# The first gate one piece later, two gates beside the fourth piece, and gate weights converted at half the rate, in a kernel of attention, Fourier mixing and two MLP stages

## The chip, the cores and the metric

The kernel runs on one core of one Trainium2 chip. The metric is device time in microseconds: 626.51 us as the median of 3 runs before the change (622.10 to 628.71). A core has TensorE (PE in the rows; its weight loads are PEld), VectorE (DVE), ScalarE (ACT), GpSimd (POOL) and SyncE (SP), each with an instruction queue of its own that it works off in order, and DMA engines that copy between HBM and the on-chip memory.

## The reference

Three blocks in a row, all in float32. For a batch of 4, with 768 time steps t:

```python
# 1. gated linear attention, 8 heads of 48
state = alpha[:, :, t, :, None] * state + einsum('bhd,bhe->bhde', k[:, :, t], v[:, :, t])
y[:, :, t] = einsum('bhd,bhde->bhe', q[:, :, t], state)
# 2. Fourier mixing and an MLP, d_model 384, hidden 1536
u = x + real(fft(fft(x, axis=1), axis=2))
un = (u - mean(u)) / sqrt(var(u) + 1e-06)
x = u + maximum(un @ w_ch1, 0) @ w_ch2
# 3. a convolution of 5 taps over time gates a value
gate = sigmoid(sum_k conv_w[k] * x shifted by k)
out = (gate * (x @ w_val)) @ w_out
```

## The kernel before, in words

**Tiling.** Attention is computed in chunks of 128 time steps, 6 chunks for each of the 4 batches. The MLP and the gate work on pieces of 256 time steps, 3 a batch, 12 in all; this text counts the pieces from the first to the twelfth. Products in the MLP and the gate are made in three parts (a high and a low part of each operand, function `mm3`, L646 to L648), so every weight is held as two arrays, and every activation is split by a copy on ScalarE and a subtraction on VectorE or GpSimd.

**Weights.** They arrive as 64-bit floats in blocks of 384 columns. `weight_parts` turns a block into its two arrays with three integer instructions on VectorE (L222, L225, L229), a copy on ScalarE (L233) and a subtraction (L238 on VectorE; in the head TensorE and ScalarE do it, L242 to L244). 24 blocks belong to the MLP; then come the convolution's taps and 6 blocks of the gate's two matrices. They pass through a buffer (`arena`) that the second batch's u takes over later.

**The head.** `first` runs the attention of the first batch and the conversion of weights in an order written by hand: one string of letters for each of 8 steps (`FIRST`), where A, B, U, S, D are parts of a chunk, w a part of a conversion, l loads, 0 to 2 the transposes of x, f to h the folds ahead of the Fourier transform, and p, r its first two parts. Then the transform of the first batch (`dft`) and the norm of its first piece.

**The main loop** (`run`) goes through the pieces. `mlp` is a generator of 24 steps: it makes the hidden layer in six pairs of 128 columns and works the second product in one pair later; each pair is evicted by ScalarE (hh, L667) and VectorE (hlo, L669). At every step the loop lets the side work go one step further (`tick`): the norm of the next piece from step 10 on, and the gate of the piece before. It also converts a weight block every second step, advances the background (`back`: attention and transform of the next batch, some 91 steps spread over a batch's three pieces by `PACE`, the parts of a chunk at the places of the letters in `ORDER`), and issues the range checks of the inputs (`check`). What is left of the gate at the end of a piece is run out before the next piece begins.

**The gate** of a piece closes the MLP (L702, L708: the product by the inverse deviation, the addition to u), splits x (L712, and L727 on GpSimd), makes the 15 taps on VectorE (L719, L721), the sigmoid on ScalarE (L729), 27 value products on TensorE, the product with the gate (L741), its split (L742 on ScalarE, L743 on GpSimd), 18 output products (L757), and two stores. It also waits until all weights are converted. The tile `ga` that holds the gate exists once.

**Attention of a chunk.** `attn_a` scans alpha on VectorE (L288 to L298), `attn_b` transposes and makes the scores on TensorE (L310, L318) with a mask (L319), `attn_c` updates the state (L335, L341 to L348), `attn_d` makes the output (L362, L368), which reads a value tile va that SyncE loads ahead (L273).

Of the kernel before, what the change touches and what calls it, by code (L numbers as in the profile page):

```python
# [9 lines left out]
F32 = mybir.dt.float32  # L10
# [3 lines left out]
AF = mybir.ActivationFunctionType  # L14
ALU = mybir.AluOpType
# [4 lines left out]
P, C = 128, 64  # L20
NT = S // P
NP = H // 2
KC = 5
NK = 256
NPC = S // NK
NF = DFF // P
KD = DM // P
# [3 lines left out]
N_CHECK = 768  # L31
N_FLAGS = 48
CHECK_FROM = 1
CHECK_STEP = 6
W_SCALE = 2.0**20
RS_SCALE = 1.3541813492306554 * 2.0**62
DEFER = 2
LAG_BG = 6
SOON = 2
BG_FROM = 5  # L40
LAG_US = 5
LAG_SS = 5
LAG_RS = 3
FIRST = ("lAwlwwlql", "llBwwlaAUSvqwll", "BwAwDwlUaqSvll", "BlwwAlwwallDUvSq", "wAylDlBwaUSwxv", "BAllUSlDlwawv", "BawDllU0lSww1lfl", "lDg2wlllplhrl")
ORDER = ".BAab..Dt..mCvc.q."
PACE = (1, 0.8, 0.95, 1.15, 0.85, 0.65, 0.95, 1.1, 1.2, 1, 1, 1)
BG_STEPS = 91
TICKS = 24
N_NORM = 10
W_DFT = (2, 0, 2, 0, 0, 0, 0, 0, 0, 1, 0)  # L50
W_CAP = 2
N_EARLY, N_SOON, N_JOBS = 18, 24, 31


# [10 lines left out]
class Main:  # L65
# [388 lines left out]


    def fold_open(self, b):
        self.us[b] = u = self.t([P, KD, S + KC - 1], "u", 2)
        self.nc.gpsimd.memset(u[:, :, 0 : KC - 1], 0.0)
        self.eo = [self.t([P, 3, 2, 193], "w", 5) for _ in range(2)]
# [228 lines left out]
        self.ch[(b, p)] = ch  # L688


    def gate(self, b, p):
        nc = self.nc
        rs = self.nm[(b, p)][2]
        ch = self.ch.pop((b, p))
        u = self.us[b]
        o = p * NK
        x2 = u[:, :, KC - 1 + o : KC - 1 + o + NK]
        gs = self.t([P, KD, NK], "ga", 1)
        tms = []
        for j in range(KD):  # L700
            tm = gs[:, j]
            nc.vector.tensor_tensor(out=tm, in0=ch[j], in1=rs, op=ALU.mult)  # L702
            tms.append(tm)
            if j == 1:
                yield
        for j in range(KD):
            eng = nc.gpsimd if b * NPC + p in ADD_POOL else nc.vector
            eng.tensor_tensor(out=x2[:, j], in0=x2[:, j], in1=tms[j], op=ALU.add)  # L708
            if j == 0:
                yield  # L710
        xh = self.pair(b * NPC + p + 2, [P, KD, NK])
        nc.scalar.activation(out=xh, in_=x2, func=AF.Copy)  # L712
        yield
        for k in range(KC):
            for j in range(KD):
                xs = u[:, j, o + k : o + k + NK]
                w = self.cw[:, j, k : k + 1]
                if k == 0:
                    nc.vector.tensor_scalar(out=gs[:, j], in0=xs, scalar1=w, scalar2=None, op0=ALU.mult)  # L719
                else:  # L720
                    nc.vector.scalar_tensor_tensor(out=gs[:, j], in0=xs, scalar=w, in1=gs[:, j],  # L721
                                                   op0=ALU.mult, op1=ALU.add)
            yield
            if k == 1:
                xl = self.pair(b * NPC + p + 2, [P, KD, NK])
                eng = nc.gpsimd if b * NPC + p in XL_POOL else nc.vector
                eng.tensor_tensor(out=xl, in0=x2, in1=xh.bitcast(F32), op=ALU.subtract)  # L727
                yield
        nc.scalar.activation(out=gs, in_=gs, func=AF.Sigmoid)  # L729
        yield  # L730
        while self.weights_left(False):
            self.weight_step()
            for _ in range(4):
                self.weight_load(True)
        gh = self.pair(b * NPC + p + 3, [P, KD, NK])
        gl = self.pair(b * NPC + p + 3, [P, KD, NK])
        for j in range(KD):
            va = self.aux()
            for k in range(KD):
                self.mm3(va[:, :NK], self.wv, slice(j * P, (j + 1) * P), (xh[:, k], xl[:, k]), k, k == 0, k == KD - 1)  # L740
            nc.vector.tensor_tensor(out=gs[:, j], in0=va[:, :NK], in1=gs[:, j], op=ALU.mult)  # L741
            nc.scalar.activation(out=gh[:, j], in_=gs[:, j], func=AF.Copy)  # L742
            nc.gpsimd.tensor_tensor(out=gl[:, j], in0=gs[:, j], in1=gh[:, j].bitcast(F32), op=ALU.subtract)  # L743
            yield
        if self.tail and b * NPC + p + 2 == B * NPC:
            self.rest = (b, p, gh, gl)
            return
        yield
        yield
        os = gs.rearrange("p a b -> p (a b)").rearrange("p (a b) -> p a b", b=DM)  # L750
        for t in range(NK // P):
            ts = slice(t * P, (t + 1) * P)
            po = self.aux()
            n = 0
            for k in range(KD):
                for lh, rh in ((gh, self.wo[0]), (gh, self.wo[1]), (gl, self.wo[0])):
                    nc.tensor.matmul(out=po[:, :DM], lhsT=lh[:, k, ts], rhs=rh[:, k, :], start=n == 0, stop=n == 8)  # L757
                    n += 1
            ob = os[:, t]
            nc.scalar.activation(out=ob, in_=po[:, :DM], func=AF.Copy)  # L760
            nc.sync.dma_start(out=self.ap["out"][b * S + o + t * P : b * S + o + (t + 1) * P, :], in_=ob)
            yield
# [115 lines left out]
    def run(self):  # L878
# [12 lines left out]
        nc = self.nc  # L891
# [18 lines left out]
        acc = 0.0  # L910
        pieces = [(b, p) for b in range(B) for p in range(NPC)]

        def tick():
            for s in list(side):
                if next(s, self) is self:
                    side.remove(s)

        for i, (b, p) in enumerate(pieces):
            n = 0
# [22 lines left out]
                tick()  # L942
            while gating and gating[0] in side:
                tick()
            self.gated = i
            if i + 1 < len(pieces):
                gating = [self.gate(b, p)]
                side.extend(gating)
        for _ in checking:
            pass  # L950
# [95 lines left out]
    def general(self, ctx):  # L1046
        nc = self.nc
        self.tail = False
        with ExitStack() as c:
            self.pools(c, "ww")  # L1050
            self.any_weights()
        xp = ctx.enter_context(self.tc.tile_pool(name="xp", bufs=1))
        self.x = xp.tile([P, NT, DM + 2], F32, name="general_x")
        self.heads = xp.tile([P, 2], F32, name="heads")
        nc.vector.memset(self.heads, 0.0)
        for j in range(2):
            nc.vector.memset(self.heads[j * 64 : j * 64 + 64, j : j + 1], 1.0)
        for b in range(B):
            with ExitStack() as c:
                self.pools(c, f"sc{b}")  # L1060
                self.scanned(b)
            with ExitStack() as c:
                self.pools(c, f"wk{b}")
                for _ in self.dft(b, False):
                    pass
                for p in range(NPC):
                    for step in (self.norm, self.mlp, self.gate):
                        for _ in step(b, p):
                            pass


@with_exitstack
# [90 lines left out]
```

## Time and profile before

| | before |
|---|---|
| median of 3 runs | 626.51 us |
| profiled execution | 625.92 us, span 624.1 us |
| TensorE busy | 584.7 us (94%) |
| VectorE busy | 409.9 us (66%) |
| ScalarE busy | 241.9 us (39%) |
| GpSimd busy | 156.3 us (25%) |
| granted clock, mean | 0.974 |

The shares are means over the span, and its stretches differ: the head with the first attention, the first two pieces with conversions beside them, the pieces with a background, and the last ones without. Where VectorE or TensorE is full is read from stretches of the trace. [...]

### The profile page before, as it was taken

To read this page: it belongs to the slowest core of one execution; us is meant where nothing else is said; L and a number is where in the kernel's file an instruction comes from. 1 tells how busy PE (TensorE), PEld (TensorE's weight loads), DVE (VectorE), ACT (ScalarE), POOL (GpSimd) and SP (SyncE) were. 2 spreads that over 40 slices of the span, in tenths; PEclk is the share of its full clock that TensorE was granted. 3 is DMA by queue.
4 is the path that set the end of the run, shared out by engine and by line. 5 is a ranking of instruction groups with operands and counts; after the bars stand their busy time and mean duration, and the time that the engine had idled before them with its cause. 6 is when DMAs were issued, how large, how long until landed. Compare 5 with 4: busy or idle time off the path is not lost.

```text
span 624.1 us, 15821 instructions
## 1 busy us (share of the span) xinstructions
PE 584.7 (94%) x6636; PEld 548.7 (88%) x6636; DVE 409.9 (66%) x881; ACT 241.9 (39%) x553; POOL 156.3 (25%) x331
## 2 busy tenths in 40 slices
PE   3788999887999998999999999999999999999996
PEld 2567888786999898999999999899998999999995
DVE  7988689999435756965753938877554536272634
ACT  2334432224453263353443243333444344435332
POOL 0010024131234043222331231322231223223130
PEclk9968998799999999999999999999999999999999
DMA  8865344573133244534313236344311122242301
GB/s 345 287 217 183 110 153 81 161 197 103 53 127 98 77 127 124 166 99 76 126 57 98 77 127 148 90 154 79 123 51 35 52 58 54 77 60 77 60 3 56
DMA packets 29601, 69.44 MB, mean 111 GB/s; under 512 B 5200, under 2 KB 15952, under 8 KB 29520
## 3 DMA queue, kind: packets, MB, share of 16 engines
q1 hardware_dynamic: 29520, 68.33, 37.6%
q8 instruction: 54, 0.88, 0.6%
q14 instruction: 27, 0.22, 0.1%
HBM read 63.59 MB, written 4.73 MB: 109 GB/s over the span
## 4 chain that ended last, share of the span: by engine, by line
PE 74%; DVE 16%; DMA 3%; POOL 2%; ACT 2%; issue 2%; SPq 0%; DVEq 0%; POOLq 0%; ACTq 0%
PE mm L646 7%; PE ch L646 7%; PE ch L647 7%; PE mm L647 7%; PE ch L648 7%; PE mm L648 7%; PE aux L757 5%; PE aux L509 4%; PE aux L554 3%; PE aux L318 2%; DVE w L295 2%; DVE w L288 2%; PE aux L646 2%; PE aux L647 2%; PE aux L648 2%
## 5 line engine op out<-in xcount | busy, mean ns | idle before, releaser
L646 PE MATMUL mm<-hl,w1h 128*128 128x256 f32 x432 | 129.6, 300 | 1.0 <-ACT hl L603 1.0
L646 PE MATMUL ch<-hh,w2h 128*128 128x256 f32 x432 | 129.7, 300 | 0.2 <-ACT hh L667 0.2
L648 PE MATMUL ch<-hlo,w2h 128*128 128x256 f32 x432 | 122.3, 283 | 1.5 <-DVE hlo L669 1.5
L648 PE MATMUL mm<-hl,w1h 128*128 128x256 f32 x432 | 123.3, 285 | 0.0
L647 PE MATMUL mm<-hl,w1l 128*128 128x256 f32 x432 | 123.2, 285 | 0.0
L647 PE MATMUL ch<-hh,w2l 128*128 128x256 f32 x432 | 122.2, 283 | 0.0
L669 DVE SCALAR_TENSOR_TENSOR hlo<-mm,hh 128x512 fp32r<-128x512 f32 x72 | 49.6, 689 | 100.7 <-ACT hh L667 100.4
L646 PEld LDWEIGHTS mm<-hl,w1h 128*128 128x128 f32 x432 | 83.3, 193 | 4.0 <-ACT hl L603 1.4
L646 PEld LDWEIGHTS ch<-hh,w2h 128*128 128x128 f32 x432 | 82.3, 190 | 2.8 <-ACT hh L667 0.4
L647 PEld LDWEIGHTS mm<-hl,w1l 128*128 128x128 f32 x432 | 83.6, 193 | 0.8
L648 PEld LDWEIGHTS mm<-hl,w1h 128*128 128x128 f32 x432 | 83.7, 194 | 0.3 <-DVE hl L606 0.3
L648 PEld LDWEIGHTS ch<-hlo,w2h 128*128 128x128 f32 x432 | 81.5, 189 | 1.9 <-DVE hlo L669 1.9
L647 PEld LDWEIGHTS ch<-hh,w2l 128*128 128x128 f32 x432 | 81.7, 189 | 0.9
L667 ACT ACTIVATE hh<-mm 128x512 fp32r<-128x512 f32 x72 | 42.6, 591 | 71.4 <-PE mm L648 71.4
L721 DVE SCALAR_TENSOR_TENSOR ga<-u,cw,ga 128x256 f32<-128x256 f32 x132 | 54.9, 476 | 0.0
L743 POOL TENSOR_TENSOR hl<-ga,hl 128x256 fp32r<-128x256 f32 x33 | 26.6, 811 | 93.2 <-ACT hl L742 92.0
L375 POOL COPY x<-x 128x2 f32<-128x2 f32 x24 | 12.6, 527 | 137.2 <-ACT x L374 137.2
L612 POOL TENSOR_TENSOR tmp<-tmp,tmp 128x256 f32<-128x256 f32 x24 | 18.1, 755 | 72.2 <-ACT tmp L611 71.3
L318 PEld LDWEIGHTS aux<-w 48*64 48x64 f32 x768 | 26.2, 144 | 9.9 <-issue 4.0
L757 PE MATMUL aux<-wvo,hl 128*128 128x384 f32 x180 | 34.8, 336 | 0.0
L318 PE MATMUL aux<-w 48*64 48x64 f32 x768 | 29.6, 231 | 4.9 <-DVE w L298 2.9
L727 POOL TENSOR_TENSOR hl<-u,hl 128x768 fp32r<-128x768 f32 x11 | 20.2, 1840 | 45.0 <-ACT hl L712 41.8
(181 smaller groups left out, 1157.6 us busy)
## 6 DMA issues: line engine op xcount, KB each, us to landing
qka<-in_qka_dram SPq DMA_DIRECT2D x23, 770.5 KB, 5.7
ck<-in_w_dram SPq DMA_DIRECT2D x24, 384.0 KB, 3.3
vu<-in_vu_dram SPq DMA_DIRECT2D x24, 192.0 KB, 3.7
u<-in_w_dram SPq DMA_DIRECT2D x12, 384.0 KB, 6.0
va<-in_va_dram SPq DMA_DIRECT2D x24, 192.0 KB, 4.1
ck<-in_al_dram SPq DMA_DIRECT2D x12, 384.0 KB, 3.5
out_dram<-ga SPq DMA_DIRECT2D x22, 192.0 KB, 1.8
w<-in_cs_dram SPq DMA_DIRECT2D x6, 579.0 KB, 5.6
```

The lines of the kernel that those rows point to most:

```text
L318: nc.tensor.matmul(out=sc[j * 64 : j * 64 + 64, cs], lhsT=kt[hs, cs], rhs=qt[hs, cs], start=True, stop=True)
L509: self.nc.tensor.matmul(out=pa[: d1 - d0, g * 193 : g * 193 + n], lhsT=self.eo[g][:, t, m, d0:d1], rhs=self.cs[g][:, t, m, :n], start=t == ...
L554: nc.tensor.matmul(out=pa[:, :385], lhsT=self.cd[:w, dt, mi, kt * P : (kt + 1) * P], rhs=pq[:w, mi, dt, :], start=dt == 0, stop=dt == 1)
L646: nc.tensor.matmul(out=out, lhsT=w[0][:, k, cols], rhs=xh, start=first, stop=False)
L647: nc.tensor.matmul(out=out, lhsT=w[1][:, k, cols], rhs=xh, start=False, stop=False)
L648: nc.tensor.matmul(out=out, lhsT=w[0][:, k, cols], rhs=xl, start=False, stop=last)
L667: nc.scalar.activation(out=hh, in_=hp, func=AF.Relu)
L669: nc.vector.scalar_tensor_tensor(out=hl, in0=hp, scalar=0.0, in1=hh.bitcast(F32), op0=ALU.max, op1=ALU.subtract)
L721: nc.vector.scalar_tensor_tensor(out=gs[:, j], in0=xs, scalar=w, in1=gs[:, j], op0=ALU.mult, op1=ALU.add)
L727: eng.tensor_tensor(out=xl, in0=x2, in1=xh.bitcast(F32), op=ALU.subtract)
L743: nc.gpsimd.tensor_tensor(out=gl[:, j], in0=gs[:, j], in1=gh[:, j].bitcast(F32), op=ALU.subtract)
L757: nc.tensor.matmul(out=po[:, :DM], lhsT=lh[:, k, ts], rhs=rh[:, k, :], start=n == 0, stop=n == 8)
```

## The change

`gate` is cut in two. `close` does the end of the MLP (L702, L708) beside the next piece as before. The rest, still called `gate`, is run by a table, `PLAN`: beside the second piece none, beside the third the first piece's gate, beside the fourth those of the second and the third piece, and from then on each beside the piece that follows, as before. The second of two gates makes its three value tiles first and splits them together at the end. Before the second batch's transform opens, all weights are converted. The intervals change: `DEFER` (steps between two conversions of the gate's blocks) from 2 to 4, `SOON` (the same for the MLP's last blocks) from 2 to 3, and several lags, the places in `ORDER`, the weights in `PACE` and the strings of `FIRST`.

```diff
-CHECK_STEP = 6
+CHECK_STEP = 5
-DEFER = 2
+DEFER = 4
-SOON = 2
+SOON = 3
-LAG_US = 5
+LAG_US = 4
-LAG_RS = 3
+LAG_RS = 4
...
-ORDER = ".BAab..Dt..mCvc.q."
-PACE = (1, 0.8, 0.95, 1.15, 0.85, 0.65, 0.95, 1.1, 1.2, 1, 1, 1)
+ORDER = ".BAab.D.t..Ccmq.v."
+PACE = (1, 0.6, 0.95, 1.2, 0.95, 0.7, 0.9, 1.1, 1.3, 1, 1, 1)
-W_DFT = (2, 0, 2, 0, 0, 0, 0, 0, 0, 1, 0)
+W_DFT = (2, 0, 1, 0, 1, 0, 0, 0, 0, 1, 0)
+PLAN = {1: (), 2: (0,), 3: (1, 2)}
...
     def fold_open(self, b):
+        while b == 1 and self.tail and self.weights_left(False):
+            self.convert_one()
...
-    def gate(self, b, p):
+    def close(self, b, p):
...
+    def gate(self, b, p, r, second=False):
+
+        nc = self.nc
+        u = self.us[b]
+        o = p * NK
+        x2 = u[:, :, KC - 1 + o : KC - 1 + o + NK]
+        gs = self.t([P, KD, NK], "ga", 1)
+        xh = self.pair(r + 1 + second, [P, KD, NK])
...
-        gh = self.pair(b * NPC + p + 3, [P, KD, NK])
-        gl = self.pair(b * NPC + p + 3, [P, KD, NK])
+            self.convert_one()
+        gh, gl = (None, None) if second else (self.pair(r + 2, [P, KD, NK]) for _ in range(2))
...
-            nc.scalar.activation(out=gh[:, j], in_=gs[:, j], func=AF.Copy)
-            nc.gpsimd.tensor_tensor(out=gl[:, j], in0=gs[:, j], in1=gh[:, j].bitcast(F32), op=ALU.subtract)
-            yield
+            if second:
+                yield
+                if j < KD - 1:
+                    continue
+                gh, gl = (self.pair(r + 2, [P, KD, NK]) for _ in range(2))
+            for i in range(KD) if second else (j,):
+                nc.scalar.activation(out=gh[:, i], in_=gs[:, i], func=AF.Copy)
+                nc.gpsimd.tensor_tensor(out=gl[:, i], in0=gs[:, i], in1=gh[:, i].bitcast(F32), op=ALU.subtract)
+                yield
...
+        def after(r):
+            yield from self.close(*pieces[r - 1])
+            for n, i in enumerate(PLAN.get(r, (r - 1,))):
+                yield from self.gate(*pieces[i], r, n > 0)
+                self.gated = i + 1
+
...
-            self.gated = i
             if i + 1 < len(pieces):
-                gating = [self.gate(b, p)]
+                gating = [after(i + 1)]
```

**Where instructions move.** On VectorE, in the second piece, between its second and third eviction of the hidden layer, there stood before (ga is the first gate's tile, w, qka, sp and st are tiles of the attention, u a staged weight block there where it is written to wvo, hlo the eviction):

```order
L669 SCALAR_TENSOR_TENSOR hlo_1768<-mm_1705,hh_1766 128x512
L719 TENSOR_SCALAR ga_1650<-u_469,cw 128x256 x3
L298 TENSOR_TENSOR w_1732<-qka_1518,w_1731 128x512
L721 SCALAR_TENSOR_TENSOR ga_1650<-u_469,cw,ga_1650 128x256 x3
L238 TENSOR_TENSOR wvo_1059<-u_103,wvo_1059 128x384
L343 TENSOR_TENSOR sp_1862<-st_1684,pend_1553 128x192
L345 TENSOR_TENSOR sp_1862<-aux_1842,sp_1862 128x192
L348 TENSOR_TENSOR st_1865<-aux_1843,sp_1862 128x192
L721 SCALAR_TENSOR_TENSOR ga_1650<-u_469,cw,ga_1650 128x256 x3
L669 SCALAR_TENSOR_TENSOR hlo_1894<-mm_1868,hh_1892 128x512
```

Now, between the same two evictions (the lines of the changed kernel are 1 to 3 higher here):

```order
L672 SCALAR_TENSOR_TENSOR hlo_1704<-mm_1681,hh_1702 128x512
L289 SCALAR_TENSOR_TENSOR w_1713<-qka_1513,ends 128x516
L293 RECIPROCAL starts<-w_1713 128x4
L294 TENSOR_TENSOR w_1714<-qka_1513,w_1713 128x512
L296 SCALAR_TENSOR_TENSOR w_1713<-qka_1513,starts 128x516
L320 TENSOR_TENSOR w_1706<-aux_1721,mask 128x512
L223 TENSOR_SCALAR u_103<-u_103 128x384
L226 SCALAR_TENSOR_TENSOR u_103<-u_103 128x384
L230 SCALAR_TENSOR_TENSOR u_103<-u_103 128x384
L239 TENSOR_TENSOR wvo_1072<-u_103,wvo_1072 128x384
L299 TENSOR_TENSOR w_1714<-qka_1513,w_1713 128x512
```

The taps of the gate are gone from here; a scan and a whole conversion stand in their place, which before stood ahead of the first of these rows.

On TensorE, where the third piece's gate ends, there stood before, in the middle of the next piece (mm and ch are products of the MLP, the tile wvo,hl rows the gate's output products):

```order
L648 MATMUL mm_3501<-hl_408_2807,w1h 128x256
L757 MATMUL aux_3524<-wvo_1059,hl_477_3322 128x384 x2
L757 MATMUL aux_3524<-wvo_1059,hl_478_3323 128x384
L757 MATMUL aux_3524<-wvo_1059,hl_477_3322 128x384 x2
L757 MATMUL aux_3524<-wvo_1059,hl_478_3323 128x384
L757 MATMUL aux_3524<-wvo_1059,hl_477_3322 128x384 x2
L757 MATMUL aux_3524<-wvo_1059,hl_478_3323 128x384
L596 MATMUL aux_3536<-tmp_3337,avg 128x256
```

The first of the output products now follow the gate's value products (hl,wvo) at once:

```order
L649 MATMUL aux_3834<-hl_515_3543,wvo_1072 128x256
L650 MATMUL aux_3834<-hl_515_3543,wvo_1072 128x256
L651 MATMUL aux_3834<-hl_532_3664,wvo_1072 128x256
L771 MATMUL aux_3855<-wvo_1072,hl_549_3845 128x384 x2
L771 MATMUL aux_3855<-wvo_1072,hl_550_3846 128x384
```

Before, products of the MLP stood between the values and the outputs of a gate; now, for this one gate, none do, and the next piece's MLP comes behind all 18 output products.

## Rows read from the trace of the kernel before

**Rows 1.** Busy time by stretch: start:end, length, engines, granted clock, DMA share, GB/s.
```profile
core 0: us, PE busy (x) PEld busy (x) DVE busy (x) ACT busy (x) POOL busy (x), PEclk, DMA share, GB/s
0.00:88.40 88.40, 67.70 (x934) 53.33 (x934) 71.67 (x153) 32.63 (x80) 7.15 (x22) 0.90 0.65 228
88.40:163.00 74.60, 64.81 (x905) 60.29 (x906) 69.03 (x139) 23.93 (x53) 22.53 (x40) 0.91 0.43 117
163.00:293.40 130.40, 127.89 (x1648) 120.49 (x1647) 78.48 (x165) 56.32 (x122) 40.28 (x84) 1.00 0.38 108
293.40:603.80 310.40, 309.72 (x3063) 300.59 (x3060) 180.59 (x401) 124.25 (x286) 86.35 (x186) 1.00 0.31 82
```

**Rows 2.** TensorE's waits, 88.4 to 163 us: total us, times, longest.
```profile
PE aux L335 <- ACT x L373: 3.3, 2, 2.4
PE aux L318 <- DVE w L602: 2.0, 1, 2.0
PE aux L362 <- DMA va<-in_va_dram: 1.7, 1, 1.7
```

**Rows 3.** VectorE's time line, 138 to 165 us: start, duration, instruction.
```profile
139.54 0.35 DVE L222 TENSOR_SCALAR u<-u 128x384 int32<-128x384 int32 x1
139.93 0.56 DVE L225 SCALAR_TENSOR_TENSOR u<-u 128x384 int32<-128x384 int32 x1
...
141.47 1.23 DVE L288 TENSOR_TENSOR_SCAN w<-qka,ends 128x516 f32<-128x516 f32 x1
...
145.73 1.37 DVE L719 TENSOR_SCALAR ga<-u,cw 128x256 f32<-128x256 f32 x3
147.02 0.68 DVE L298 TENSOR_TENSOR w<-qka,w 128x512 f32<-128x512 f32 x1
147.62 1.27 DVE L721 SCALAR_TENSOR_TENSOR ga<-u,cw,ga 128x256 f32<-128x256 f32 x3
148.81 0.55 DVE L238 TENSOR_TENSOR wvo<-u,wvo 128x384 fp32r<-128x384 f32 x1
...
158.29 0.68 DVE L298 TENSOR_TENSOR w<-qka,w 128x512 f32<-128x512 f32 x1
...
160.08 0.41 DVE L741 TENSOR_TENSOR ga<-aux,ga 128x256 f32<-128x256 f32 x1
```

**Rows 4.** A gate's end: groups of 163 to 293.4 us, and the chain.
```profile
L742 ACT ACTIVATE hl<-ga 128x256 fp32r<-128x256 f32 x8 | 3.3, 411 | 5.8 <-DVE ga L741 5.8
L743 POOL TENSOR_TENSOR hl<-ga,hl 128x256 fp32r<-128x256 f32 x8 | 6.6, 831 | 18.3 <-ACT hl L742 18.3
171.00 1.57 PE aux L757 x9
```

**Rows 5.** The chain of waits, 60 to 90 us: start, us, what.
```profile
61.16 0.68 PE aux L468 x6
...
62.46 0.54 PE aux L368 x32
...
64.57 1.30 PE mm L509 x8
```

**Rows 6.** VectorE beside GpSimd: time lines, and all taps (ns min/median/max).
```profile
114.15 1.74 POOL L612 TENSOR_TENSOR tmp<-tmp,tmp 128x256 f32<-128x256 f32 x2 [12.19 <-ACT tmp L611]
114.32 0.97 DVE L225 SCALAR_TENSOR_TENSOR u<-u 128x384 int32<-128x384 int32 x1
L721 DVE SCALAR_TENSOR_TENSOR ga<-u,cw,ga x132: 469/476/482, 147.6 to 590.5; 128x256 f32<-128x256 f32 x132
```

**Rows 7.** The value load: issues (count, KB, median us to landing), and the chain.
```profile
va<-in_va_dram SPq DMA_DIRECT2D x24, 192.0 KB, 4.1
238.37 6.20 DMA va<-in_va_dram
```

More of the change, by code (lines that the diff above doesn't have):

```diff
@@ L33 @@
 CHECK_FROM = 1
-CHECK_STEP = 6
+CHECK_STEP = 5
 W_SCALE = 2.0**20
 RS_SCALE = 1.3541813492306554 * 2.0**62
-DEFER = 2
+DEFER = 4
 LAG_BG = 6
-SOON = 2
+SOON = 3
 BG_FROM = 5
-LAG_US = 5
+LAG_US = 4
 LAG_SS = 5
-LAG_RS = 3
-FIRST = ("lAwlwwlql", "llBwwlaAUSvqwll", "BwAwDwlUaqSvll", "BlwwAlwwallDUvSq", "wAylDlBwaUSwxv", "BAllUSlDlwawv", "BawDllU0lSww1lfl", "lDg2wlllplhrl")
-ORDER = ".BAab..Dt..mCvc.q."
-PACE = (1, 0.8, 0.95, 1.15, 0.85, 0.65, 0.95, 1.1, 1.2, 1, 1, 1)
+LAG_RS = 4
+FIRST = ("llAwlwwlqlll", "lllBwllwAaUqSvwl", "wBAwDwllUlalvqSl", "lBwAwwallvDUSq", "wAyDlBwaUSwxvl", "BUwAlllllSlDwvaw", "lBaDUwll0lSww1f", "Dgllpwll2lhlr")
+ORDER = ".BAab.D.t..Ccmq.v."
+PACE = (1, 0.6, 0.95, 1.2, 0.95, 0.7, 0.9, 1.1, 1.3, 1, 1, 1)
 BG_STEPS = 91
@@ L710, in gate @@
                 yield
-        xh = self.pair(b * NPC + p + 2, [P, KD, NK])
+    def gate(self, b, p, r, second=False):
[5 more added lines that the diff above has]
+        xh = self.pair(r + 1 + second, [P, KD, NK])
         nc.scalar.activation(out=xh, in_=x2, func=AF.Copy)
@@ L724, in gate @@
             if k == 1:
-                xl = self.pair(b * NPC + p + 2, [P, KD, NK])
+                xl = self.pair(r + 1 + second, [P, KD, NK])
                 eng = nc.gpsimd if b * NPC + p in XL_POOL else nc.vector
@@ L731, in gate @@
         while self.weights_left(False):
-            self.weight_step()
-            for _ in range(4):
-                self.weight_load(True)
-        gh = self.pair(b * NPC + p + 3, [P, KD, NK])
-        gl = self.pair(b * NPC + p + 3, [P, KD, NK])
+            self.convert_one()
+        gh, gl = (None, None) if second else (self.pair(r + 2, [P, KD, NK]) for _ in range(2))
         for j in range(KD):
@@ L1066, in general @@
                 for p in range(NPC):
-                    for step in (self.norm, self.mlp, self.gate):
+                    for step in (self.norm, self.mlp, self.close):
                         for _ in step(b, p):
                             pass
+                    for _ in self.gate(b, p, b * NPC + p + 1):
+                        pass
 @with_exitstack
```

## The prediction

> **What bounds the kernel now.** I read the busy time by stretch first, with the span cut where the program changes its nature [rows 1]. From 293.4 to 603.8 us TensorE is busy 309.72 of 310.4 us at granted clock 1.00: nothing can be gained there by moving work, only lost. From 163.0 to 293.4 us it is still TensorE, 127.89 of 130.4 us, with VectorE at 78.48. Between 88.4 and 163.0 us it is the other way round: VectorE is busy 69.03 of 74.6 us, TensorE 64.81 at a mean clock of 0.91. That is the first piece of the MLP and two thirds of the second, where VectorE has the weights of the gate to convert, the scans of the second batch's attention and the first gate. The head before 88.4 us is mixed, TensorE 67.70 and VectorE 71.67 of 88.4.
>
> Then the waits of TensorE in the middle stretch [rows 2]: 3.3 us for ScalarE to free a bank of PSUM, 2.0 us for VectorE in one transposed product, 1.7 us for a load. The waits are small because TensorE reaches most of them late. What is long is VectorE's own queue: its time line [rows 3] stands without a gap from 138 to 160 us while a weight, a scan and a tap of the convolution take turns.
>
> So there is work that can move: VectorE is full until 163 us and 60% busy (78.48 of 130.4) in the next stretch, while TensorE is the bound there. I sum against the profiled execution, 625.92 us with a span of 624.1; the median of the three runs, 626.51, lies 0.6 above it.
>
> **What leaves the stretch from 88.4 to 163.0 us.** I cut both orders at the same place, the fourth eviction of the second piece's hidden layer, and count VectorE's instructions before it. Missing after the change are:
> - the first gate's 15 taps and one product with its values. Three first taps start at 145.73 and the next instruction at 147.02, 1.29 us; three later ones take 147.62 to 148.81, 1.19 us, four times [rows 3]. With the product, 0.4 us, 6.5 us.
> - three weight blocks and one more subtraction, since a block is now converted every fourth step of the MLP, not every second. A block runs from 139.54 to 141.47, 1.93 us [rows 3]; the subtraction is a quarter of it: 6.3 us.
> - the end of one attention chunk (one product, three state updates), 158.29 to 160.08, 1.8 us [rows 3], because the background is paced slower there.
>
> Together 14.6 us, 33 instructions of 138. None disappears; all stand again between there and the first eviction of the fifth piece. VectorE would be busy 54.4 us. If its idle share of today stays (74.6 - 69.03 = 5.6 us) the stretch lasts 60.0 us.
>
> TensorE has 64.81 us there less what leaves it, 9 products of the gate and 16 small ones of the attention, 1.8 us: 63.0 us, if its clock falls as often as now. If it never fell, 64.81 x 0.91 - 1.8 = 57.2 us would do. On the other side, the waits of TensorE that no VectorE work causes, 3.3 and 1.7 us [rows 2], come on top of 63.0: 68.0. **I take 63.0**, TensorE's own work at today's clock, since it lies above VectorE's 60.0 and is made of the row nearest to it. That is 11.6 us less than 74.6, with 57.2 to 68.0 as ends (17.4 and 6.6 less).
>
> The clock first as the rows have it: mean 0.91 where TensorE waits for VectorE, 1.00 in the two stretches where it is 98% and 99.8% busy [rows 1]. [...]
>
> **What arrives from 163.0 to 293.4 us.** VectorE gets 78.48 + 14.6 = 93 us in some 132: covered by TensorE, at no cost. TensorE gets its 1.8 us back, and it is the bound: **+1.8 us**.
>
> **Where the cover is thin: the end of the fourth piece.** Its side work is now one closing, one gate and a second gate, 35 steps against the 24 of a piece. The rest is run out with no MLP work between. The order shows it: the second gate's 27 value products and the 18 output products stand back to back. Between them ScalarE must copy (0.41 us) and GpSimd subtract three times (0.83 us each) [rows 4], 2.9 us to the last piece, and the last of the first nine output products needs it. Nine take 1.57 us [rows 4]; so 2.9 + 0.17 - 1.57, **+1.5 us** of TensorE idle. Below, nothing, if GpSimd's tiles come while TensorE is still at the values. Above: VectorE may be late with the taps ahead of it.
>
> [...] Beside GpSimd's two additions at 114.15 us a VectorE instruction of the conversion took 0.97 us; the same one at 139.93, alone, 0.56 [rows 3, 6]. The taps never did so: 132 of them lie between 469 and 482 ns [rows 6], but almost none runs beside a GpSimd addition today. [...] If it held for all twelve two-input taps of the second gate, they would take 12 x 0.40 x (0.97 / 0.56 - 1) = 3.5 us more. [...]
>
> **The head.** One group of transposes now stands behind the first eight products of the Fourier transform, not ahead of them. They waited for the last attention chunk's evictions: TensorE leaves that chunk at 63.0 (62.46 + 0.54) and starts the transform at 64.57 [rows 5]. Starting it at once gives 1.57; the six transposes, 0.68 [rows 5], then stand inside: **-0.9 us**, on the chain. The other head edits (a state product ahead of weight products, a mask product behind a conversion) let VectorE run ahead and then wait for TensorE elsewhere; I take 0, and 1.5 us either way.
>
> **Edits at nothing.** The number of the range checks, of the norms' additions and of the background's steps is unchanged; their new places lie under TensorE's 309.72 of 310.4 us [rows 1]. The value load of the attention is issued four background steps ahead of its use, not five. If that cover went, TensorE would wait in each chunk; priced below.
>
> **Sum:** -11.6 + 1.8 + 1.5 - 0.9 = -9.2; 625.92 - 9.2 = **616.7 us**.
>
> **The rivals.**
> 1. *The bound only changes hands.* TensorE and VectorE come out nearly equal (63.0 and 60.0), and each waits for the other in turn: a scan for a product, a product for an eviction. Then the stretch takes 68.0, the piece's end 5.0 and the head nothing: 625.92 - 6.6 + 1.8 + 5.0 = 626.1. For it: the waits there today are of that kind [rows 2]. Against: today VectorE has only 5.6 us of idle time in 74.6 with such dependences. Half of the 9.4 us between this and the forecast already gives 621. Within 1%.
> 2. *The clock holds too.* 57.2 us instead of 63.0: 616.7 - 5.8 = 610.9. For it, the 1.00 of the full stretches [rows 1]. Against, the clock also fell where TensorE was mostly busy.
> 3. *Slower: the value load comes late.* It is landed 4.1 us after its issue in the median, but 6.2 us in the longest link of the chain [rows 7], where TensorE waited; 91 steps are spread over three pieces, some 140 us, so a step is about 1.5 us, the lead falls from 7.6 to 6.1 us, and SyncE issues in order behind other waits. If all 18 background chunks lost 1.5 us, it would cost 27 us: 644. From 0.9 us a chunk (16 us in all) the kernel is over 1% slower. Against: the median leaves 2 us, and of the waits of today only the longest loads are left.
> 4. *The conversion is not really deferred*: the program must finish all weights before the second batch's transform opens, since they share a buffer. The order shows one block left to force there, 2 us at most, so this only shades rival 1.
>
> **Chances.** A change below 1%, 6.3 us, cannot be told from none here: faster means below 620.2, slower above 632.8. The forecast, 613 to 620: 0.54. Rival 2, below 613: 0.18. Rival 1 with the part of 4, 620 to 633: 0.21. Rival 3: 0.07. So faster 0.72, same 0.21, slower 0.07. The range: from the sum with 57.2 us and 1.5 us more from the head, 609, to rival 1 at 626; below and above lie some 2 in 10. The likeliest cases' own range, forecast and rival 2, is 609 to 620.
>
> **What would show it.** In the profile of the changed kernel: the stretch from the first hidden eviction to the tenth near 63 us with VectorE near 54; TensorE's share there above 95% and no half clock for much longer than now; at the end of the fourth piece a wait of 1 to 2 us of the output products for GpSimd's subtraction; the transform starting some 1.5 us earlier than the transposes before it allow today; waits for the value load no more than 5 us in all. Wrong would be: TensorE idle for VectorE in the second piece as before, waits for the value load in most chunks, or more than 5 us of idle time where the fifth piece starts.

## The result, and the profile after

The changed kernel takes 616.83 us (median of 4 runs, 613.6 to 618.44) where the kernel before took 625.51 beside it: a ratio of 0.984, 95% interval 0.980 to 0.988. Timed once more in the third study below it had 614.06 us and 0.981, 0.978 to 0.984. The forecast was 616.7 us, faster. The profiled execution took 617.39 us with a span of 615.6.

Busy time by stretch, cut at the same places of the program as [rows 1] (start:end, length, TensorE, weight loads, VectorE, ScalarE, GpSimd, granted clock, DMA share, GB/s). The granted clock is the share of its full clock that the profile records as granted to TensorE; in the traces of both kernels every record of it is 1.00 or 0.50, and 0.50 is what half clock means here.

```profile
core 0: us, PE busy (x) PEld busy (x) DVE busy (x) ACT busy (x) POOL busy (x), PEclk, DMA share, GB/s
0.00:86.30 86.30, 63.37 (x934) 50.55 (x934) 71.54 (x152) 32.64 (x81) 7.73 (x22) 0.94 0.67 234
86.30:149.00 62.70, 57.12 (x877) 53.97 (x881) 54.64 (x106) 20.23 (x48) 19.48 (x38) 0.95 0.43 126
149.00:285.80 136.80, 132.79 (x1693) 124.69 (x1684) 96.13 (x198) 61.76 (x134) 47.49 (x85) 0.99 0.40 118
285.80:595.10 309.30, 309.14 (x3053) 300.14 (x3053) 177.56 (x401) 118.66 (x279) 87.62 (x186) 1.00 0.27 78
```

The second line is the one to read: 62.70 us where there were 74.6, and VectorE at 54.64 where there were 69.03. The third line gives half of that back: 136.80 for 130.4, with TensorE at 132.79 for 127.89.

TensorE's waits in the second stretch, which answer to [rows 2] (total us, times, longest):

```profile
PE aux L363 <- DMA va<-in_va_dram: 2.5, 1, 2.5
PE aux L319 <- DVE w L299: 1.9, 1, 1.9
PE aux L363 <- DVE sp L342: 1.1, 1, 1.1
```

The longest is now a load (va, the values of the attention), which had 1.7 us in this stretch before [rows 2]. What the clock does behind it is seen in two cuts of the busy time:

```profile
121.00:130.50 9.50, 7.69 (x113) 7.19 (x112) 9.19 (x20) 2.58 (x7) 2.21 (x5) 1.00 0.64 113
130.50:137.40 6.90, 6.22 (x84) 6.16 (x85) 5.10 (x9) 2.35 (x6) 1.76 (x3) 0.51 0.55 211
```

TensorE waits from 128.7 to 131.2 us; at 130.5 us the granted clock falls from 1.00 to 0.50 and stays there for 6.8 us. The products of the MLP start 0.21 us apart in that time and 0.12 us apart right behind it.

The end of the double gate on TensorE and GpSimd, which answers to [rows 4] (start, us, instruction, idle time before it):

```profile
277.56 0.62 PE L771 MATMUL aux<-wvo,hl 128*128 128x384 f32 x2 [0.44 <-ACT hl L756]
278.37 3.42 PE L771 MATMUL aux<-wvo,hl 128*128 128x384 f32 x16 [0.19 <-POOL hl L757]
```

0.6 us of waiting, not 1.5. The head's chain, which answers to [rows 5], has the transform (L512) right behind the last attention chunk (L369), and the transposes (L471) inside:

```profile
61.14 0.47 PE aux L369 x32
61.61 1.48 PE mm L512 x8
63.09 1.30 PE ch L512 x8
64.39 0.68 PE aux L471 x6
```

The taps, which answer to [rows 6], are no slower in the mean, 475 ns for the 132 with two inputs. None of these ran beside one of GpSimd's subtractions of a whole tile; three ran beside its products of two columns, at 477 to 479 ns:

```profile
L732 DVE SCALAR_TENSOR_TENSOR ga<-u,cw,ga 128x256 f32<-128x256 f32 x132 | 54.8, 475 | 0.0
```

The value load of [rows 7] has a median of 4.0 us to landing, 4.1 before.

### The profile page after: what moved, and what is told of

Its sections match the earlier page's. It is cut to its first block, busy times and chain, and to the rows that moved or that the text cites. A ratio compares the mean times of both kernels' runs of the same rounds, so it can differ in the third digit from the quotient of the medians.

```text
span 615.6 us, 15843 instructions
## 1 busy us (share of the span) xinstructions
PE 577.0 (94%) x6636; PEld 543.3 (88%) x6636; DVE 410.0 (67%) x881; ACT 238.0 (39%) x553; POOL 162.3 (26%) x331
## 4 chain that ended last, share of the span: by engine, by line
PE 79%; DVE 10%; DMA 4%; POOL 2%; issue 2%; ACT 1%; SPq 0%; DVEq 0%; ACTq 0%; POOLq 0%
PE ch L649 8%; PE mm L649 8%; PE ch L650 7%; PE ch L651 7%; PE mm L651 7%; PE mm L650 7%; PE aux L771 5%; PE aux L512 4%; PE aux L557 3%; DMA va<-in_va_dram 3%; PE aux L319 2%; PE aux L649 2%; PE aux L650 2%; PE aux L651 2%; PE aux L363 2%
## 5 line engine op out<-in xcount | busy, mean ns | idle before, releaser
L649 PE MATMUL ch<-hh,w2h 128*128 128x256 f32 x432 | 128.3, 297 | 0.0
L649 PEld LDWEIGHTS mm<-hl,w1h 128*128 128x128 f32 x432 | 82.3, 191 | 4.0 <-ACT hl L606 1.4
L651 PEld LDWEIGHTS mm<-hl,w1h 128*128 128x128 f32 x432 | 82.3, 191 | 0.3 <-DVE hl L609 0.3
L376 POOL COPY x<-x 128x2 f32<-128x2 f32 x24 | 14.4, 600 | 131.5 <-ACT x L375 131.4
L705 DVE TENSOR_TENSOR ga<-ch,rs 128x256 f32<-128x256 f32 x33 | 12.9, 418 | 32.0 <-PE ch L651 24.8
L771 PEld LDWEIGHTS aux<-wvo,hl 128*128 128x128 f32 x180 | 30.6, 188 | 1.6 <-POOL hl L757 0.9
```

The costliest lines, as they stand in the source:

```text
L376: nc.gpsimd.tensor_copy(out=xt[:, 1 : DM + 1 : DM - 1], in_=xt[:, 0:1].to_broadcast([P, 2]))
L649: nc.tensor.matmul(out=out, lhsT=w[0][:, k, cols], rhs=xh, start=first, stop=False)
L651: nc.tensor.matmul(out=out, lhsT=w[0][:, k, cols], rhs=xl, start=False, stop=last)
```

## The experiments

There were three studies: e6, e7, e8 and e3 in the first, f1, f3, e2 and e4 in the second, g0, f2, g1 and f7 in the third. Every kernel was timed beside the kernel before on the same chip, so kernels of different studies are compared by their ratios. Diffs are against the changed kernel, and `...` marks what is left out of them. The theory: VectorE's relief shortens the stretch, and part of it comes back behind. The rival: the orders do it, or the head. All kernels together first, in us; the cuts are the first, tenth, twenty-fifth and last hidden eviction in the trace of each; the idle columns are TensorE's (length less busy time):

| kernel | ratio, interval | head | stretch: length, VectorE, idle | second: length, TensorE, idle | rest | tail |
|---|---|---|---|---|---|---|
| before | | 88.4 | 74.6, 69.03, 9.8 | 130.4, 127.89, 2.5 | 310.4 | 20.4 |
| changed | 0.984, 0.980–0.988 | 86.3 | 62.7, 54.64, 5.6 | 136.8, 132.79, 4.0 | 309.3 | 20.5 |
| g0_again | 0.981, 0.978–0.984 | 87.4 | 60.5, 54.60, 4.6 | 134.6, 131.12, 3.5 | 309.5 | 20.2 |
| e6_plan_only | 1.001, 0.999–1.003 | 88.5 | 67.9, 63.40, 8.3 | 136.6, 131.19, 5.4 | 310.2 | 20.3 |
| e7_defer_only | 0.998, 0.996–1.001 | 88.9 | 77.6, 69.23, 11.1 | 127.3, 124.54, 2.8 | 310.4 | 20.5 |
| e8_orders_only | 0.997, 0.995–0.999 | 86.6 | 76.0, 67.05, 14.6 | 129.8, 128.79, 1.0 | 309.8 | 20.4 |
| e3_orders_back | 1.001, 1.000–1.003 | 88.7 | 65.6, 58.45, 6.9 | 141.6, 133.98, 7.6 | 310.4 | 20.2 |
| f1_head_back | 0.980, 0.977–0.983 | 90.8 | 61.3, 54.48, 3.0 | 136.1, 132.73, 3.4 | 309.4 | 20.1 |
| f2_lags_back | 0.987, 0.984–0.990 | 89.5 | 59.8, 54.74, 3.2 | 138.9, 133.49, 5.4 | 309.9 | 20.1 |
| f3_bg_back | 0.989, 0.985–0.992 | 85.8 | 63.6, 55.89, 5.3 | 139.2, 131.63, 7.6 | 310.5 | 20.1 |
| e2_rate_back | 0.983, 0.980–0.986 | 89.7 | 65.6, 60.52, 6.2 | 134.7, 131.31, 3.4 | 309.5 | 20.2 |
| e4_va_early | 0.976, 0.973–0.979 | 85.1 | 58.9, 54.45, 4.7 | 135.5, 132.81, 2.7 | 309.0 | 20.4 |
| g1_va_rate | 0.982, 0.980–0.984 | 86.4 | 65.3, 60.45, 8.1 | 133.0, 130.76, 2.2 | 309.1 | 20.2 |
| f7_va_double | 0.987, 0.984–0.990 | 88.5 | 59.1, 54.50, 3.8 | 125.3, 123.35, 2.0 | 323.8 | 20.4 |

The ratio is of several runs, the stretches of one execution: kernels with the same head show it at 85.1 to 89.7 us, with 10.2 us at half clock in the shortest and 20.5 in the longest. So a difference of a microsecond or two in one stretch is not read as an effect.

**e6_plan_only**: the gates by the new table; the rate, SOON, the three lags and all orders as before (the diff shows two of them).

```diff
-DEFER = 4
+DEFER = 2
...
-ORDER = ".BAab.D.t..Ccmq.v."
+ORDER = ".BAab..Dt..mCvc.q."
```

> Only the new table of gates: the first gate beside the third piece, two beside the fourth; conversions, lags and all orders as before. Theory (VectorE's queue in the stretch from the first to the tenth hidden eviction sets its length): 6.5 us of VectorE work leave the stretch, which falls from 74.6 to about 68 us; of that 2 to 4 us come back behind it. About 4 us faster than before, ratio 0.994. Rival (the orders made the gain): ratio 1.000, the stretch above 73 us. Rival (the clock made it): the stretch shortens only as far as its time at half clock does, from 13.6 us.

626.53 us, no change where a gain of 0.6% had been expected. The stretch came as the count of VectorE's instructions said, and nearly all of it went again:

```profile
88.50:156.40 67.90, 59.57 (x889) 55.19 (x889) 63.40 (x122) 21.39 (x51) 20.14 (x38) 0.95 0.45 128
156.40:293.00 136.60, 131.19 (x1667) 122.63 (x1665) 85.63 (x181) 58.85 (x126) 43.51 (x85) 1.00 0.36 107
```

VectorE lost 5.6 us and the stretch 6.7. The second stretch is 6.2 longer: TensorE has 3.3 us more to do there, and 2.9 us more of idle time, of which its waits name

```profile
PE aux L771 <- ACT hl L756: 1.8, 1, 1.8
PE aux L363 <- DMA va<-in_va_dram: 1.7, 1, 1.7
PE ch L651 <- DVE hlo L672: 0.8, 1, 0.8
PE aux L512 <- POOL w L487: 0.6, 1, 0.6
```

The second and the fourth stood there before, with 1.9 and 0.6 us. The first and the third are new, 2.6 us, and belong to the double gate and the piece beside it: VectorE reaches them late.

**e7_defer_only**: the weights at half the rate; the table empty, so each gate at its old place, and orders, lags and SOON as before.

```diff
-PLAN = {1: (), 2: (0,), 3: (1, 2)}
+PLAN = {}
...
-ORDER = ".BAab.D.t..Ccmq.v."
+ORDER = ".BAab..Dt..mCvc.q."
```

> Only the interval of the gate's conversions from 2 to 4 steps; gates and orders as before. Theory: the first gate still stands in the second piece and must wait for all weights, so it runs the deferred conversions in one lump ahead of the tenth eviction: VectorE's sum in the stretch stays 70.3 us. No change, ratio 0.998 to 1.004, the stretch at 74 to 76 us. Rival (half the rate is the gain by itself): ratio 0.990, the stretch near 69 us.

624.66 us, no change. Its VectorE is as full in the stretch as before, 69.23 us: with the gate at its old place the interval moves nothing out of it.

**e8_orders_only**: the new orders with the old table and rate.

```diff
-DEFER = 4
+DEFER = 2
-PLAN = {1: (), 2: (0,), 3: (1, 2)}
+PLAN = {}
```

> Only the orders and lags of the change (strings of the head, letters and pace of the background, norm, checks, and the MLP's last weights every third step); gates as before, the gate's conversions every second step. Theory: 1.7 us of VectorE work leave the stretch and the head is 2 us shorter: 3 to 4 us faster, ratio 0.994, the head at 86.3 us instead of 88.4. Rival (the orders made the gain): ratio 0.988 or less.

623.58 us, 0.3% less, half of what had been expected. Table alone nothing, rate alone at most 0.4% by its interval, orders alone 2 us: none of them alone has the change's 9 to 12 us.

**e3_orders_back**: table and rate new; SOON, the three lags and all orders as before.

```diff
-ORDER = ".BAab.D.t..Ccmq.v."
+ORDER = ".BAab..Dt..mCvc.q."
-PACE = (1, 0.6, 0.95, 1.2, 0.95, 0.7, 0.9, 1.1, 1.3, 1, 1, 1)
+PACE = (1, 0.8, 0.95, 1.15, 0.85, 0.65, 0.95, 1.1, 1.2, 1, 1, 1)
...
```

> The new table of gates and the conversions every fourth step, with all orders and lags as before. Theory: 10.9 us of VectorE work leave the stretch, which falls to 64 to 65 us, the head stays at 88.4; with 3 to 5 us coming back behind it, 5 to 7 us faster than before, ratio 0.990; the table and the interval together give more than the sum of each alone. Rival (the orders made the gain): ratio 0.998.

627.34 us, where a per cent less was expected. The stretch is 9.0 shorter and the second stretch 11.2 longer. In the latter TensorE stands idle 7.6 us, and runs its output products of the double gate mostly at half clock (3.4 us from 286.2), 5.21 us for 18, behind a wait three times as long:

```profile
285.85 5.21 PE L771 MATMUL aux<-wvo,hl 128*128 128x384 f32 x18 [1.76 <-ACT hl L756]
```

**f1_head_back, f2_lags_back, f3_bg_back**: one of the three groups of orders undone. In f1 the head's, FIRST and W_DFT:

```diff
...
-W_DFT = (2, 0, 1, 0, 1, 0, 0, 0, 0, 1, 0)
+W_DFT = (2, 0, 2, 0, 0, 0, 0, 0, 0, 1, 0)
```

In f2 the lags:

```diff
-CHECK_STEP = 5
+CHECK_STEP = 6
...
-LAG_US = 4
+LAG_US = 5
...
-LAG_RS = 4
+LAG_RS = 3
```

In f3 the background's, ORDER and PACE, with the two lines shown for e3.

> The changed kernel with the order of the head as it was before; the background's order, the lags, the gates' table and the deferred weights stay changed. Theory (each edit has its place: the head's order is worth its own 2 us and nothing else; the return behind the stretch is held down by the background's order): the head grows from 86.3 to 88.4 us, the stretch stays at 62 to 64 us, the second stretch at 136 to 138 us, so 2 us slower than the changed kernel, 619 us, ratio 0.989 to the kernel before. Rival A (the head's order sets where everything behind it falls, and it alone keeps the return small): the second stretch goes to 140 to 142 us as in the run with all old orders, 624 us or more, ratio 0.998 or above. Rival B (the head's 2 us are lost again behind, since TensorE then waits longer for VectorE): 617 us, ratio 0.985, as the changed kernel.

> The changed kernel with the old order and the old pace of the background attention; the head's order, the lags, the gates' table and the deferred weights stay changed. Theory (the background's pace decides what VectorE has in hand where the double gate ends): head 86.3 us, stretch 64 to 66 us, second stretch 140 to 142 us with 1.5 us or more of idle TensorE and half clock at the double gate's output products, in all 622 to 624 us, ratio 0.995 to 0.998 to the kernel before. Rival A (head's order alone): 617 us as the changed kernel, second stretch 136 to 138. Rival B (the orders act only all together, each half undone loses all of it): 626 us or more.

> The changed kernel with the old lags: five background-free steps ahead of a norm's mean and three around its scale, not four and four, and a range check's passes spread over six steps, not five; orders, table and deferred weights stay changed. With all orders, pace and lags old the ratio was 1.001, with the background's order and pace alone old 0.9885, with the head's alone old 0.980. Theory (it is the background's order and pace together with the lags that hold the return down, so the lags must carry what is left, some 0.8 per cent): ratio 0.990 to 0.994, second stretch 139 us or more, with TensorE waiting for VectorE or GpSimd where the second batch's transform opens or where the fifth piece starts. Rival A (each part costs little alone, the three overlap): ratio 0.980 to 0.986, second stretch 135 to 138 us.

**g0_again** is the changed kernel unaltered, since f1 had come out no slower than it.

> The changed kernel once more, unaltered, beside the kernels below, since with the head's order undone it came out at a ratio of 0.980 where the changed kernel had 0.984 from four runs. Theory (the head's order is worth nothing in the time; the 2 us of the one profile are the clock of that execution, since another kernel with the same head took 89.7 us for it): ratio 0.980 to 0.984, head between 86 and 90 us in its profile. Rival (undoing the head's order is a gain of 2 us): ratio 0.983 to 0.986.

Undoing the head costs nothing (0.980; the changed kernel 0.984 and 0.981), undoing the lags 0.3 to 0.6%, undoing the background 0.5 to 0.8%, by ratios whose intervals overlap that of the changed kernel's first timing and lie just above that of its second. All together, in e3, cost 1.7 to 2%; but e3 also has the old SOON, which no kernel undid by itself. So the rival that the head does it falls. My sizes for f1 (0.989), f2 (0.990 to 0.994) and f3 (0.995 to 0.998) were too large: none of the three groups by itself carries the gain. The stretches came nearer: f3's second stretch of 139.2 us and its wait of 1.6 us at the output products. TensorE's waits of f3 in the two stretches show what the background's order and pace had prevented:

```profile
PE aux L512 <- POOL w L487: 2.8, 3, 1.7
PE aux L771 <- ACT hl L756: 1.6, 1, 1.6
PE ch L651 <- DVE hlo L672: 1.4, 2, 1.2
```

Against 2.0 (for VectorE, L489), 0.4 and 0.2 in the changed kernel: the opening of the second batch's transform, the double gate's end and the piece beside it. Idle time is 7.6 us in the second stretch in both kernels with the old background and the new rate (f3, e3); with the new background and the same table and rate it is 2.7 to 4.0, and 5.4 where the lags are old (f2).

**e2_rate_back** (a weight block every second step again) and **e4_va_early** (the letter m, the load of the values, two steps earlier), and both in **g1_va_rate**. The first two:

```diff
-DEFER = 4
+DEFER = 2
```

```diff
-ORDER = ".BAab.D.t..Ccmq.v."
+ORDER = ".BAab.D.tm..Ccq.v."
```

> The changed kernel with a weight block converted every second step again, not every fourth, all else as changed. By the count of instructions VectorE has 62.2 us before the tenth hidden eviction, not 55.8. Theory (the stretch follows VectorE's load, and what was left in the stretch need not be done behind it): stretch 66 to 68 us, second stretch 132 to 134 us, since no folds and conversions are late for the second batch's transform (its wait of 2 us and the half clock behind it, 1.7 us, go): 616 to 619 us, ratio 0.984 to 0.990. Rival (the deferring is needed for the gain, since only with it VectorE leaves the path): stretch 66 to 68, second stretch still 136 to 137, 621 to 623 us, ratio 0.993 to 0.996.

> The changed kernel with the load of the attention's values issued two background steps earlier (six steps ahead of its use), all else as changed. In the changed kernel TensorE waits 5.8 us in four places for this load, 2.5 us of it at 128.7 us with 6.8 us of half clock right behind, which costs 3.4 us more. Theory (the value load is late because of its issue): no wait for it over 0.5 us, no half clock from 130.5 us, stretch 57 to 60 us, 611 to 614 us, ratio 0.977 to 0.982. Rival A (the load is hidden behind VectorE anyway, so another wait takes its place, for a scan's state or an eviction): stretch 61 to 63, 616 to 618 us, ratio 0.984 to 0.987. Rival B (the load waits in SyncE's queue behind others and lands as late as before, or collides with the head's loads): waits for it of 1 us and more stay, 617 us or more.

> The changed kernel with the attention's values loaded two background steps earlier and the weights converted every second step again. With the early load alone the ratio was 0.976, with the rate alone 0.983. In the profile of the latter TensorE waited 5.3 us for the values, in three places, and 10.2 us of half clock stood behind two of them. Theory (deferring the conversion buys nothing once the gate is moved; the waits for the load are what both kernels lose to): no wait for the values, stretch 58 to 62 us, ratio 0.973 to 0.978. Rival (with the load early VectorE is the bound of the stretch again, and its 6.4 us more show): stretch 64 to 67 us, ratio 0.980 to 0.985.

e2: 617.25 us, as the changed kernel. The wait of 1.6 us where the second batch's transform opens, which I had expected to go, stayed. Its waits for the values in the stretch:

```profile
PE aux L363 <- DMA va<-in_va_dram: 4.2, 2, 2.4
```

e4: 611.21 us, 0.976, the fastest of all, and faster than the kernel before and the changed one (its interval, 0.973 to 0.979, just reaches that of g0, 0.978 to 0.984). Its stretch has no wait for the values and never half the clock:

```profile
85.10:144.00 58.90, 54.22 (x873) 51.18 (x877) 54.45 (x106) 20.09 (x48) 20.28 (x38) 1.00 0.44 135
```

What is left in its waits is VectorE, and the other operand's load (vu) once:

```profile
PE aux L319 <- DVE w L299: 1.9, 1, 1.9
PE aux L336 <- DMA vu<-in_vu_dram: 1.6, 1, 1.6
PE aux L363 <- DVE sp L342: 1.1, 1, 1.1
```

g1 was expected at 0.973 to 0.978 and came to 0.982: the theory that the deferring buys nothing fell, the rival was right. Its stretch:

```profile
86.40:151.70 65.30, 57.22 (x895) 53.51 (x896) 60.45 (x120) 21.00 (x51) 19.26 (x38) 1.00 0.41 132
```

The value waits of e2 there are gone and the clock is at 1.00, and still it is 65.3 us, e2's 65.6: VectorE's 60.45 with 4.9 on top. Waits and half clock had lain in time that VectorE needed anyway. e4, with VectorE at 54.45, has 4.5 on top. So of these two rates the early load gains only at the one where VectorE has been relieved further.

**f7_va_double**: e4 with the double gate a piece later.

```diff
-PLAN = {1: (), 2: (0,), 3: (1, 2)}
+PLAN = {1: (), 2: (0,), 3: (1,), 4: (2, 3)}
```

> The changed kernel with the attention's values loaded two background steps earlier, and the second and third gate run one piece later again: one gate beside piece 3, two beside piece 4 (the fifth piece). With the early load alone the ratio was 0.976 and the second stretch 135.5 us. Theory (the second stretch is TensorE's own work with 3 to 4 us of waits; the gate's products move behind the fifth piece, where TensorE is busy 309 of 309 us): second stretch 3 to 5 us shorter, the rest 3 to 5 us longer, ratio 0.975 to 0.978. Rival A (the double gate beside piece 3 loads VectorE so that the transform's folds come late): the wait of 1.6 us where the transform opens goes, and the half clock behind it, ratio 0.970 to 0.974. Rival B (the second batch's pieces need the buffers of the gates, so the delay shows as waits in the rest): ratio 0.980 or above.

619.09 us, 0.987: my theory and rival A are refuted (the wait where the transform opens stayed at 1.6 us), and rival B has the time, by another cause: VectorE and not a buffer. The second stretch is 10.2 us shorter than in e4, the rest 14.8 longer. The net 4.6 us answer to one wait where the two gates end; the head of this execution is 3.4 us longer as well, at 20.5 us of half clock:

```profile
314.55 5.15 PE L771 MATMUL aux<-wvo,hl 128*128 128x384 f32 x18 [4.63 <-ACT hl L756]
```

Ahead of it VectorE has the folds of the third batch's transform (L489) between the taps, and is late:

```profile
311.36 1.27 DVE L732 SCALAR_TENSOR_TENSOR ga<-u,cw,ga 128x256 f32<-128x256 f32 x3
312.55 0.62 DVE L489 TENSOR_TENSOR w<-f 128x191 f32<-128x191 f32 x2
313.54 1.09 DVE L749 TENSOR_TENSOR ga<-aux,ga 128x256 f32<-128x256 f32 x3 [0.37 <-ACT ga L740]
```

## Why the prediction was right, and where it was not

The time and the sign were right, and so was the mechanism that relief of VectorE shortens the stretch and part of it comes back behind. Which engine then sets the stretch was wrong, and the return was sized at half. That the sum came within a microsecond is luck: against its -9.2 stand 8.5 us of span, with 3.1 us more coming back, 1.2 more gained in the head, 1.1 in the rest, where I had nothing, and 0.3 in the stretch. In the profiled execution:

- **The stretch, -11.6.** Measured -11.9, and -14.1 in g0. VectorE's load was right to 0.2 us (54.4; 54.64). The length was taken for the wrong reason, and that it came so near is luck. I took TensorE's own work at today's clock, 63.0, and put TensorE's share above 95%; TensorE is busy 57.12 us, 91%, at a clock of 0.95. The value that I had worked out beside it, VectorE with today's idle share, 60.0, is what the runs follow: VectorE's busy time lies 4.5 to 5.9 us under the length in the kernel before and in g0, e6, f2, e2, e4, g1 and f7. In the changed kernel's profile it is 8.1 us, with 2.5 us of waiting for the values and 6.8 us of half clock in the stretch; in g0 the wait is 1.5 us, in e4 there is none. In the other kernels more lies on top (6.8 to 9.0 in e7, e8, e3, f1 and f3), with 3.4 to 20.5 us of half clock in the stretch. That the half clock is what lies on top is not shown: e2 has 13.4 us of it and only 5.1 on top.
- **The clock.** I kept its loss out of the forecast, as a rival. Less of it was lost: the stretch's clock is 0.91 before, 0.95, 0.97 (g0) and 1.00 (e4), where TensorE is busy 87, 91, 92 and 92% of the time. In these four a fuller TensorE goes with a higher clock; two others show that the busy share alone does not tell it: g1 has 1.00 at 88%, f1 0.92 at 95%. And TensorE's 54 to 57 us are not the stretch: VectorE is. Rival 2's clock of 1.00 came in e4 and g1, its stretch of 57.2 us in none: it is 58.9 and 65.3 there.
- **What arrives, +1.8.** Measured 4.9 of busy time: too small. 1.7 of it is half clock behind the transform's opening (my estimate: half of the 3.4 us at a clock of 0.50), which g0 does not have; without it the term is 3.2 (131.12 - 127.89). I counted 25 products that leave the stretch. By the rows 28 leave it, and the second stretch shows 45 to 47 more than before, 10 of them out of the rest, where TensorE has 0.6 us less; 7 to 9 are not accounted for.
- **The double gate's end, +1.5.** Measured 0.6. The first ScalarE copy started 0.5 us ahead of the output products, and these could begin on tiles that were ready, so only 0.2 us were left to wait for GpSimd. The range that I had named, from nothing, holds it. Rival 1 has 5.0 us here, which is 1.5 and the 3.5 that I had estimated for twelve slower taps. No run shows that term: the wait here is 0.6 us, and a tap takes 475 ns, 476 before [rows 6], but no two-input tap ran beside a subtraction of a whole tile, so the taps do not test it. The trace shows slower instructions beside GpSimd elsewhere: first taps, which I had left out though one in [rows 3] already took 0.85 us beside GpSimd's subtraction (0.34 in the median beside none), and folds of the transform, as the next item tells. With the old orders (e6, e3) the wait was 1.8 us and 0.8 ahead of it; f7's 4.6 us shows what the place costs when VectorE is late.
- **A wait that was not in the sum:** the second batch's transform waits 2.0 us for VectorE's folds (L489) at its opening, where 0.64 stood before. 1.6 of it is one fold that ran beside GpSimd's split of the first gate (L738), which the new table has put there. Two folds take 0.61 us away from it and 2.22 where one runs beside it:

```profile
172.53 0.61 DVE L489 TENSOR_TENSOR w<-f 128x191 f32<-128x191 f32 x2
175.64 2.22 DVE L489 TENSOR_TENSOR w<-f 128x191 f32<-128x191 f32 x2
```

```profile
175.72 1.93 POOL L738 TENSOR_TENSOR hl<-u,hl 128x768 fp32r<-128x768 f32 x1
```

```profile
178.28 2.18 PE L512 MATMUL aux<-w,w 128*97 128x192 f32 x6 [1.60 <-DVE w L489]
```

All eight kernels with the first gate beside the third piece and the new background (the changed one, g0, f1, f2, e2, e4, g1, f7) show the same fold at 1.96 to 1.97 us beside the same split and the same wait of 1.6 us; none of the others does. In e3 and f3 the transform waits 2.8 us for GpSimd's own copies there, in e6 0.6. The fold is an instruction that I had not looked at. I had called what arrives on VectorE covered by TensorE. In the mean of a stretch it is (96.13 of 136.80), at this opening and at the double gate's end it is not. With the half clock behind it (1.7 us) this wait is half of the 6.4 us by which the second stretch grew. No kernel took the split away from the folds and left the rest as it was.
- **The head, -0.9.** The start of the transform came as told: 61.61, where the chunk ends. The stage is 2.1 shorter here and 1.0 in g0, at 17.1 us of half clock as before. f1 shows no cost in the runs, within some 2 us; so -0.9 is neither shown nor excluded.
- **Edits at nothing.** The rest became 1.1 us shorter, with 10 products less. The lags, which I had put at nothing, are worth 0.3 to 0.6%; f2's profile puts most of that into the second stretch, 138.9 us.
- **Rival 3**, the late load, did not happen: the waits for it are 5.8 us in four places, and 4.2 in g0, where the kernel before had 5.3 in three. I had put 5 as the limit without that row. That e4 gains 0.5 to 0.8% by an earlier load is a gain beside the change, not a loss that the change brought.

What the prediction had not seen is that the parts are worth little apart. It put 11.6 us on the stretch, most of it for the table and the rate, and gave the orders of the head 0.9; table and rate with the old orders and the old SOON are no faster than before. By e6 and e3 the reason is the same term: what returns. It was 3.3 in the sum, is 6.4 in the changed kernel, and is 11.2 in e3. The forecast held because the orders, the lags and SOON together kept the return down, which it had not priced. Lags and background cost 0.3 to 0.6 and 0.5 to 0.8% apart, and 1.7 to 2 in e3, together with the head and the old SOON. What makes the difference is not settled: no kernel undid two groups at a time, and none SOON alone.

## What to carry to other kernels

Work moved off a full engine shortened the stretch by about what that engine lost (VectorE 14.4 us and the stretch 11.9 in the changed kernel, 14.4 and 14.1 in g0, 5.6 and 6.7 in e6), and took the other engines' part of the same work along: add the moved products where they arrive, in a stretch that their engine bounds. Then look at the points where the moved work is due, and at what it runs beside there, not at the mean of the stretch; in this kernel the orders around those points decided whether anything was left. A wait that was removed paid only where the engine that bounds the stretch was not using the time: the early load was worth 0.5 to 0.8% with VectorE at 54.5 us and nothing with it at 60.5.

## What the hardware showed that was not expected

The first tap of a gate, which reads one tensor, is slower beside GpSimd's subtraction, as the fold above is, while a hidden eviction beside it is not. Beside 1.83 us of GpSimd three first taps take 1.95, 0.65 in the mean; over all 33 the mean is 470 ns:

```profile
264.95 1.95 DVE L730 TENSOR_SCALAR ga<-u,cw 128x256 f32<-128x256 f32 x3
```

```profile
264.39 1.83 POOL L738 TENSOR_TENSOR hl<-u,hl 128x768 fp32r<-128x768 f32 x1
```

In the trace of the changed kernel 6 first taps lie almost wholly beside a GpSimd subtraction or addition, with a median of 957 ns, and 24 beside none, with 341. In the kernel before it is 8 with 950 and 22 with 342, so this did not come with the change. The hidden eviction, with two inputs, one of them in PSUM, takes 692 (27 of them) and 691 ns (42). Scans with two inputs have a median of 1.22 to 1.23 us either way, but four of the 48 took 1.62 to 1.78 us, all beside GpSimd.

Half clock stands at the end of waits that are no longer than 1.6 to 2.5 us (those from 128.7 and 176.7 us in the changed kernel), and not of all of them: at the same wait of 1.6 us in g0 the clock stayed at 1.00:

```profile
172.00:182.00 10.00, 7.95 (x54) 7.46 (x53) 9.10 (x19) 2.40 (x4) 4.29 (x5) 1.00 0.45 127
```
